# Seven products for two more pairs, and half of the layer norm on ScalarE: a fused FNet and GLU kernel on one core

## The chip, the core and the metric

The kernel runs on one core of one Trainium2 chip. Its engines work side by side, each through its own queue in order: TensorE (PE) multiplies, VectorE (DVE), ScalarE (ACT) and GpSimd (POOL) work on elements, SyncE (SP) and POOL issue DMAs, and 16 DMA engines carry those. The metric is the device time of one execution in microseconds (us); the time of a kernel is the median of its runs.

## The reference

All tensors are fp32.

```python
# S = 2048, D = 512, F = 1792
xn = layernorm(x)                                   # rows of 512, eps 1e-5, no weights
a, b = xn @ dft_hid_re.T, xn @ dft_hid_im.T
s = dft_seq_re @ a - dft_seq_im @ b
g = silu((sigmoid(xn @ w_gate) * (xn @ w_up)) @ w_down)
out = x + s * g
```

## The kernel before

All products are made of fp32 numbers split in two parts, hi and lo (`split`, L71 to L73: ACT copies the hi part, DVE subtracts it to get the lo part), and each product is three matmuls (`mm3`, L75): hi*hi, hi*lo, lo*hi. So an operand costs one ACT and one DVE instruction before PE can use it.

The work has three stages: the GLU with its gate (x by `w_gate` and `w_up`, then by `w_down`), the DFT along the sequence, and the DFT along the hidden dimension with the last product and sum. The change lies in the first.

The GLU works on the two halves h of the 2048 rows (1024 each) and on seven pairs g of F-columns (256 each). A **block** is one (h, g), in the order of `BLOCKS` (L27): after (0, 0), which is done while the first half is normalised, come (0,1), (0,2), (0,3), (0,4), (1,4) and so on. A block's product is done in Strassen's manner, as seven products in place of eight, and each of the seven is one **unit** of PE work: units 0 to 6 are block (0,1), 7 to 13 block (0,2), 14 to 20 block (0,3), 21 to 27 block (0,4), 28 to 34 block (1,4), the first one of the second half. A unit's 12 matmuls go to two banks of PSUM (ga and ua, or b and c), and after some units ACT copies the banks out (`snap`, `seed`) or DVE adds them (`plus`).

The product with `w_down` of a block's result (the **down product**) is done in pieces, each behind the main product of a unit of the next block. There are two ways. `Plain` (L314) has four pieces of 12 matmuls, and needs the weights and the four result tiles split. `Seven` (L388) has seven pieces of 6 matmuls, in Strassen's manner too, and needs four sums of results (`sums`), four differences of weights (`Down.diffs`), and seven results and two weight tiles split. The pieces of `Seven` lie in all seven units, from the second unit of the next block to the first of the one behind. Each piece ends in `gather` (L298): ACT copies its two banks into a page (L302), and POOL issues a DMA which adds the page to a tensor in DRAM (`g_part`, L304; the first one of each only writes, L307). Two of the seven go to `g_part` 0 one after the other, two to 2, two to 3. Pairs 1 and 2 of the first half are `Plain`, all others `Seven` (`SEVEN_FROM`, L987).

The layer norm of the second half's rows is made during the first blocks: `fetch` loads tiles 8 to 15 of 128 rows, two to a page; `norm_a` (L157) makes mean and variance on DVE (bn_stats, bn_aggr) and the scale on POOL; `norm_b` (L171) normalises the tile on DVE; `store_xn` (L197) stores it for the next stage, from POOL's queue. The GLU needs the second half turned, with rows along the free axis: `turned_half` (L175) stores mean and scale (`moments`) to DRAM from POOL's queue as single numbers (`store`, L183), loads them back spread over all partitions (`both`), and applies them to the turned x (`raw`, from `x_t`) on DVE in four steps of 128x1024 (`step`, L188).

What stands in the order: the program is written out unit by unit. `sooner(n, f)` puts f ahead of unit n, `after(n, f)` behind it; each unit's operands are loaded 5 units ahead and split 2 units ahead. Every engine then keeps that order. All tiles in SBUF are **pages** out of one pool of 54 slots of 4 KB per partition. Which slot a new page takes is fixed when the program is built; its first writer waits on the chip until the last reader of the page before it is done. For a page that was gathered, that reader is a DMA, and the wait ends when the DMA has landed.

Of the kernel before, what the change touches and what calls it, by code (L numbers as in the profile page):

```python
# [9 lines left out]
F32 = mybir.dt.float32  # L10
F32R = mybir.dt.float32r
AF = mybir.ActivationFunctionType
ALU = mybir.AluOpType
ADD, SUB = ALU.add, ALU.subtract

P = 128
S, D, F = 2048, 512, 1792
# [4 lines left out]
KH = NS // NH  # L22
NT = S // 512
SB = 512
EPS = 1e-5
# [1 line left out]
SCRATCH = 4096  # L27
BLOCKS = ((0, 1), (0, 2), (0, 3), (0, 4), (1, 4), (1, 5), (0, 5), (0, 6), (1, 6), (1, 0), (1, 1), (1, 2), (1, 3))
FIRST_TURNED = 1, 4
SEVEN_FROM = 3  # L30
SHARED = 4, 5, 6
SPLIT_AHEAD = 2
LOAD_AHEAD = 5
# [3 lines left out]
def fnet_glu_kernel(ctx: ExitStack, tc: tile.TileContext, x, x_t, c_re, c_im, w_h, w_gu, w_down, out):  # L37
    nc = tc.nc
    PSUM = bass.MemoryType.PSUM

    const = ctx.enter_context(tc.tile_pool(name="const", bufs=1))
# [5 lines left out]
    def page(shape, dtype=F32R):  # L47
        return pages.tile([P, *shape], dtype, name="page")

    def bank(tag):  # L50
        return banks.tile([P, 512], F32, name=tag, bufs=2 if tag == "pd" else 1)
# [5 lines left out]
    mhalf = const.tile([P, 1], F32, name="mhalf")  # L57
    nc.gpsimd.memset(mhalf, -0.5)
    warm = const.tile([P, 1], F32, name="warm")
    nc.scalar.activation(warm, mhalf, AF.Sigmoid)  # L60
    moments = const.tile([P, 2, KH], F32, name="moments")
    m_part = dram.tile([2, 2, SB], F32, name="m_part")
    xn_part = dram.tile([2, 2, 2, P, 4, D // 2], F32, name="xn_part")
    g_part = [dram.tile([P, 2, SB], F32, name=f"g_part{i}") for i in range(2 * NT)]
# [67 lines left out]
    def add(needs, run):  # L132
        units.append((needs, run))
# [4 lines left out]
    def after(n, f):  # L138
        extra.setdefault(n, []).append(f)

    def sooner(n, f):
        early.setdefault(n, []).append(f)


    xs = {}
# [7 lines left out]
            nc.sync.dma_start(xs[i + j], x[(i + j) * P : (i + j + 1) * P, :])  # L153

    st_of = {}

    def norm_a(i):  # L157
        st = stat.tile([P, 6], F32, name="st")
        mv = stat.tile([P, 2], F32, name="mv")
        rs = stat.tile([P, 2], F32, name="rs")  # L160
        nc.vector.bn_stats(st, xs[i])
        nc.vector.bn_aggr(mv, st)
        mean, scale = mv[:, 0:1], rs[:, 1:2]
        if i >= KH:
            mean, scale = (moments[:, m, i - KH : i - KH + 1] for m in range(2))
            nc.gpsimd.tensor_scalar(mean, mv[:, 0:1], 0.0, None, op0=ALU.add)
        nc.gpsimd.tensor_scalar(rs[:, 0:1], mv[:, 1:2], EPS, None, op0=ALU.add)
        nc.gpsimd.tensor_tensor(scale, rs[:, 0:1], mhalf, op=ALU.pow)
        st_of[i] = mean, scale

    def norm_b(i):  # L171
        mean, scale = st_of.pop(i)
        nc.vector.tensor_scalar(xs[i], xs[i], mean, scale, op0=ALU.subtract, op1=ALU.mult)

    def turned_half(n, b, at):  # L175

        both = Load(m_part[b].rearrange("m t -> (m t)").partition_broadcast(P).rearrange("p (m t) -> p m t", m=2), [2, SB])
        raw = [Load(x_t[(2 + b) * 2 + j], [2, SB]) for j in range(2)]

        def store():  # L180
            at = slice(b * SB // P, (b + 1) * SB // P)
            for m in range(2):
                nc.gpsimd.dma_start(m_part[b, m].rearrange("(o p) -> p o", p=P), moments[:, m, at])  # L183

        def step(j, m):
            v = xraw[1, j, b] = raw[j].load()
            by = both.load()[:, m, :].unsqueeze(1).to_broadcast([P, 2, SB])
            nc.vector.tensor_tensor(v, v, by, op=(SUB, ALU.mult)[m])  # L188

        after(n, store)  # L190
        sooner(at[0] - 2, both.load)
        for i in range(4):
            if i % 2 == 0:
                sooner(at[i] - 4, raw[i // 2].load)
            after(at[i], lambda i=i: step(*divmod(i, 2)))
# [118 lines left out]
    class Plain:  # L314


        items, at = range(4), (1, 3, 4, 6)
# [70 lines left out]
    class Seven:  # L388


        items, at = SEVEN, range(7)
# [52 lines left out]
    def block(h, w, made, before, job, late):  # L444

        s, ps = job.s, {}
        n = len(units)
        if not made:
            for i, v in zip((-3, 0, 1, 3), w["s"]):
                sooner(n + i, v.get)  # L450

        def snap(k):
            s[k] = page([2, SB], F32)
            for m, c in enumerate("gu"):
                nc.scalar.activation(s[k][:, m, :], ps[c + "a"], AF.Copy)

        def seed():

            for c in "gu":
                ps[c + "b"] = bank(c + "b")  # L460
                nc.scalar.activation(ps[c + "b"], ps[c + "a"], AF.Copy)

        def plus(k):
            for m, c in enumerate("gu"):
                nc.vector.tensor_add(s[k][:, m, :], s[k][:, m, :], ps[c + "c"])

        def gate(k, tag=None):
            if tag:
                s[k] = page([2, SB], F32)
            nc.scalar.activation(s[k][:, 0, :], ps["g" + tag] if tag else s[k][:, 0, :], AF.Sigmoid)  # L470

        def times(k, tag=None):
            nc.vector.tensor_mul(s[k][:, 0, :], s[k][:, 0, :], ps["u" + tag] if tag else s[k][:, 1, :])

        tail = {1: seed, 6: lambda: snap(2), 7: lambda: (snap(3), plus(3)), 3: lambda: plus(2)}
        CH = {1: "a", 5: "c", 2: "b", 6: "a", 7: "a", 4: "a", 3: "c"}

        def unit(k, d):
            first = k in (1, 5)
            for m, c in enumerate("gu"):  # L480
                tag = c + CH[k]
                if first:
                    ps[tag] = bank(tag)
                product(k, ps[tag], w, h, m, first)
            if k in tail:
                tail[k]()
            if d:
                d[0].run(d[1])
            if k in (2, 4):
                gate({2: 1, 4: 4}[k], CH[k])  # L490
            if k in (7, 3):
                gate({7: 3, 3: 2}[k])
            if k == 4:
                times(4, "a")

        for i, k in enumerate((1, 5, 2, 6, 7, 4, 3)):
            if i == 1:
                waiting.extend((before, d) for d in before.items)
            d = waiting.pop(0) if waiting and i in waiting[0][0].at else None
            add([xop[h, k], w[k]] + (d[0].needs(d[1]) if d else []), lambda k=k, d=d: unit(k, d))  # L500
        sooner(n + 3, lambda: times(1, "b"))
        sooner(n + 5, lambda: times(3))
        sooner(n + 7, lambda: times(2))
        job.spread(n, late)
        return job
# [470 lines left out]
    with tc.manual_schedule():  # L976
        job, begin = start(0, 0)
        for i in range(KH):
            after(i // 2, lambda i=i: store_xn(i))
        last = None  # L980
        for h, g in BLOCKS:
            made = g == last
            if not made:
                w, wd, last = w_operands(g), Down(g), g
            if (h, g) == FIRST_TURNED:
                turned_at = len(units)
            job = block(h, w, made, job, Seven(h, wd, made) if h or g >= SEVEN_FROM else Plain(h, g), g in SHARED)  # L987
        for i in range(0, KH, 2):
            a, b = ((2, 9), (4, 10), (7, 12), (8, 14))[i // 2]
            if i >= 4:  # L990
                sooner(a - 4, lambda i=i: fetch(KH + i))
            for j in (i, i + 1):
                after(a, lambda j=j: norm_a(KH + j))
                after(b, lambda j=j: norm_b(KH + j))
                after(b + 1, lambda j=j: store_xn(KH + j))
        n = turned_at
        turned_half(4, 0, (n - 18, n - 17, n - 14, n - 4))
        turned_half(8, 1, (n - 13, n - 12, n - 10, n - 3))
        for i, k in {-7: 1, -2: 2, 0: 3, 2: 4}.items():
            after(n + i, lambda k=k: x_sum(1, k))  # L1000
        for i, k in {-8: 1, -5: 5, -2: 2, 0: 6, 1: 7, 3: 4}.items():
            sooner(n + i, xop[1, k].get)
        sums_ahead(diffs, xn_blocks(0), s_part[0], (n + 15, n + 16, n + 17, n + 18), 3)
        sums_ahead(diffs, xn_blocks(1), s_part[1], (n + 28, n + 29, n + 30, n + 31), 3)
        sums_ahead(sums, c_blocks(0, 0), t_part[0], (n + 32, n + 33, n + 34, n + 35), 3)
        seq_units(job)
        hidden_units()
        begin()
        for n, (needs, run) in enumerate(units):
            now[0] = n  # L1010
            for f in early.get(n, []):
                f()
            for k in range(n, min(n + LOAD_AHEAD + 1, len(units))):
                for p in units[k][0]:
                    p.load()
            for k in range(n, min(n + SPLIT_AHEAD + 1, len(units))):
                for p in units[k][0]:
                    p.get()
            run()
            for f in extra.get(n, []):  # L1020
                f()
# [52 lines left out]
```

## Time and profile before

| | us |
|---|---|
| median of 3 runs | 813.05 (810.47 to 814.35) |
| profiled execution | 809.47 |
| its span, first to last instruction | 807.6 |
| PE busy | 801.0 (99%) |
| DVE busy | 639.7 (79%) |
| ACT busy | 496.9 (62%) |
| POOL busy | 150.8 (19%) |

The mean granted TensorE clock of the profiled execution is 0.999 of full speed. Busy time is the time in which an engine has an instruction under way; the share is of the span. A name such as page or g_part stands for all tiles of that name. The DMA share is the mean busy share of the 16 DMA engines, and it can pass 1, since an engine has several packets under way. The queue q0 holds what POOL issues, q1 what SP issues. "To landing" is the time from a DMA's issue to its last byte.

### The profile page before, as it was taken

Reading aid. Unit: us, or ns where it says so; the run is one execution under the profiler, and the core shown is the slowest. Engines: PE = TensorE matmul, PEld = TensorE weight load, DVE = VectorE, ACT = ScalarE, POOL = GpSimd, SP = SyncE. Lnnn points to the kernel's source line nnn. Section 1 sums busy time; section 2 is a strip of 40 time slices with the busy share of each in tenths; the row PEclk is TensorE's granted clock in tenths of the full one; section 3 lists DMA queues with packets and bytes.
Section 4 is the critical chain, followed back from the end, with each engine's and each line's share of the span. In section 5 each row is a group of like instructions: output and inputs, shape, how many; then the busy total and the mean of one; then the engine's idle time right before and its main releaser. Section 6 shows DMA issues by size and latency. Waiting matters only on the chain.

```text
span 807.6 us, 10288 instructions
## 1 busy us (share of the span) xinstructions
PE 801.0 (99%) x3630; PEld 665.3 (82%) x3630; DVE 639.7 (79%) x803; ACT 496.9 (62%) x761; POOL 150.8 (19%) x222
## 2 busy tenths in 40 slices
PE   9999999999999999999999999999999999999997
PEld 7988888888888888888888888888888888888886
DVE  6897879876776787787798796888888876986946
ACT  4674657777676678778877765445445545536360
POOL 3146321221222222131211100011101210001201
PEclk9999999999999999999999999999999999999999
DMA  8366994987899998989899988277929994799976
GB/s 278 140 225 110 219 263 72 182 159 156 240 253 226 290 295 236 236 199 175 236 294 311 282 294 293 98 284 286 329 85 324 350 389 141 244 337 386 314 254 104
DMA packets 55651, 193.62 MB, mean 240 GB/s; under 512 B 6320, under 2 KB 6576, under 8 KB 55600
## 3 DMA queue, kind: packets, MB, share of 16 engines
q0 software_dynamic: 24624, 85.48, 45.4%
q1 hardware_dynamic: 30896, 107.43, 37.7%
q8 instruction: 28, 0.46, 0.2%
q14 instruction: 23, 0.19, 0.1%
q10 hardware_dynamic: 80, 0.07, 0.0%
HBM read 110.62 MB, written 85.99 MB: 243 GB/s over the span
## 4 chain that ended last, share of the span: by engine, by line
PE 98%; DMA 1%; DVE 0%; ACT 0%; SPq 0%; issue 0%
PE pd L77 7%; PE pd L76 7%; PE pd L78 7%; PE ga L76 6%; PE ga L77 6%; PE ua L77 6%; PE ga L78 6%; PE ua L78 6%; PE ua L76 6%; PE gc L77 4%; PE uc L77 3%; PE gc L78 3%; PE uc L78 3%; PE gc L76 3%; PE uc L76 3%; PE ub L77 3%
## 5 line engine op out<-in xcount | busy, mean ns | idle before, releaser
L73 DVE TENSOR_TENSOR page<-page 128x1024 fp32r<-128x1024 f32 (+1 forms) x351 | 332.4, 976 | 110.3 <-ACT page L72 109.2
L72 ACT ACTIVATE page<-page 128x1024 fp32r<-128x1024 f32 (+1 forms) x351 | 284.2, 857 | 93.6 <-DVE page L124 74.2
L124 DVE TENSOR_TENSOR page<-page 128x1024 f32<-128x1024 f32 (+2 forms) x216 | 188.8, 893 | 0.9 <-DMA page<-in_w_gu_dram 0.3
L302 ACT ACTIVATE page<-pd 128x512 f32<-128x512 f32 x178 | 104.6, 598 | 67.5 <-PE pd L78 54.6
L304 POOL DMA_DIRECT2D g_part<-page x81 | 71.6, 949 | 282.5 <-ACT page L302 166.4
L76 PE MATMUL pd<-page 128*128 128x512 f32 x234 | 91.0, 389 | 0.0
L77 PE MATMUL pd<-page 128*128 128x512 f32 x234 | 91.0, 389 | 0.0
L78 PE MATMUL pd<-page 128*128 128x512 f32 x234 | 91.0, 389 | 0.0
L76 PE MATMUL ga<-page 128*128 128x512 f32 x200 | 78.2, 391 | 0.0
L77 PE MATMUL ga<-page 128*128 128x512 f32 x200 | 77.9, 389 | 0.0
L76 PE MATMUL ua<-page 128*128 128x512 f32 x200 | 77.8, 389 | 0.0
L77 PE MATMUL ua<-page 128*128 128x512 f32 x200 | 77.8, 389 | 0.0
L78 PE MATMUL ga<-page 128*128 128x512 f32 x200 | 77.8, 389 | 0.0
L78 PE MATMUL ua<-page 128*128 128x512 f32 x200 | 77.8, 389 | 0.0
L76 PEld LDWEIGHTS pd<-page 128*128 128x128 f32 x234 | 43.9, 188 | 9.2
L78 PEld LDWEIGHTS pd<-page 128*128 128x128 f32 x234 | 43.9, 188 | 9.1
L77 PEld LDWEIGHTS pd<-page 128*128 128x128 f32 x234 | 43.9, 188 | 9.1
L77 PE MATMUL gc<-page 128*128 128x512 f32 x124 | 48.3, 390 | 0.0
L76 PE MATMUL gc<-page 128*128 128x512 f32 x124 | 48.2, 389 | 0.0
L78 PE MATMUL gc<-page 128*128 128x512 f32 x124 | 48.2, 389 | 0.0
L76 PE MATMUL uc<-page 128*128 128x512 f32 x124 | 48.2, 389 | 0.0
L78 PE MATMUL uc<-page 128*128 128x512 f32 x124 | 48.2, 389 | 0.0
(133 smaller groups left out, 1302.3 us busy)
## 6 DMA issues: line engine op xcount, KB each, us to landing
g_part<-page POOLq DMA_DIRECT2D x89, 512.0 KB, 8.3
page<-f_part SPq DMA_DIRECT2D x36, 512.0 KB, 6.1
page<-in_c_re_dram SPq DMA_DIRECT2D x34, 512.0 KB, 6.2
page<-in_c_im_dram SPq DMA_DIRECT2D x33, 512.0 KB, 7.0
f_part<-page POOLq DMA_DIRECT2D x28, 512.0 KB, 6.9
page<-in_w_gu_dram SPq DMA_DIRECT2D x22, 512.0 KB, 7.0
page<-xn_part SPq DMA_DIRECT2D x14, 512.0 KB, 5.6
page<-in_w_down_dram SPq DMA_DIRECT2D x11, 512.0 KB, 7.9
```

The costliest lines, as they stand in the source:

```text
L72: nc.scalar.activation(hi, src, AF.Copy)
L73: nc.vector.tensor_tensor(lo, src, hi.bitcast(F32), op=SUB)
L76: nc.tensor.matmul(ps, ws[0], ms[0], start=first, stop=False, skip_group_check=go_on)
L77: nc.tensor.matmul(ps, ws[0], ms[1], start=False, stop=False, skip_group_check=go_on)
L78: nc.tensor.matmul(ps, ws[1], ms[0], start=False, stop=last, skip_group_check=go_on)
L124: (engine or nc.vector).tensor_tensor(dst, a, b, op=op)
L302: nc.scalar.activation(pg[:, o, :], po, AF.Copy, scale=float(sign))
L304: nc.gpsimd.dma_start(g_part[i], pg, accum_op=ADD)
```

## The change

Pairs 1 and 2 of the first half become `Seven` too (`SEVENS`). The statistics of tiles 8 to 15 are made by ACT in two passes with a running sum, each 128x512 and written to a page that nobody reads: the sum (from which POOL makes mean and minus mean), then the sum of the squared differences (from which POOL makes scale and minus mean times scale). The tiles are normalised by ACT with scale and bias. The passes come a unit or two sooner than the statistics did, normalising and storing come later (tiles 8 and 9 after unit 11, not 9; 10 and 11 after 14, not 10; 12 and 13 after 28, not 12; 14 and 15 after 30, not 14), and the steps of `turned_half` move: units 10, 11, 12, 13 in place of 10, 11, 14, 24, and 15, 17, 22, 24 in place of 15, 16, 18, 25. Lines behind L27 stand up to 18 lines lower in the changed file: L302 and L304 become L319 and L321.

```diff
-SEVEN_FROM = 3
+SEVENS = 1, 2, 3, 4, 5, 6
...
-    moments = const.tile([P, 2, KH], F32, name="moments")
+    moments = const.tile([P, 6, KH], F32, name="moments")
...
+    unused = Value([], lambda: page([D], F32))
...
         mean, scale = mv[:, 0:1], rs[:, 1:2]
-        if i >= KH:
-            mean, scale = (moments[:, m, i - KH : i - KH + 1] for m in range(2))
-            nc.gpsimd.tensor_scalar(mean, mv[:, 0:1], 0.0, None, op0=ALU.add)
         nc.gpsimd.tensor_scalar(rs[:, 0:1], mv[:, 1:2], EPS, None, op0=ALU.add)
         nc.gpsimd.tensor_tensor(scale, rs[:, 0:1], mhalf, op=ALU.pow)
         st_of[i] = mean, scale
+
+    def second_stats(i, m):
+
+        def at(k):
+            return moments[:, k, i - KH : i - KH + 1]
+
+        if m == 0:
+            nc.scalar.activation(unused.get(), xs[i], AF.Identity, accum_out=at(2))
+            nc.gpsimd.tensor_scalar(at(0), at(2), 1.0 / D, None, op0=ALU.mult)
+            nc.gpsimd.tensor_scalar(at(3), at(2), -1.0 / D, None, op0=ALU.mult)
+        else:
+            nc.scalar.activation(unused.get(), xs[i], AF.Square, bias=at(3), accum_out=at(4))
+            nc.gpsimd.tensor_scalar(at(4), at(4), 1.0 / D, EPS, op0=ALU.mult, op1=ALU.add)
+            nc.gpsimd.tensor_tensor(at(1), at(4), mhalf, op=ALU.pow)
+            nc.gpsimd.tensor_tensor(at(5), at(3), at(1), op=ALU.mult)
+
+    def second_norm(i):
+        scale, bias = (moments[:, m, i - KH : i - KH + 1] for m in (1, 5))
+        nc.scalar.activation(xs[i], xs[i], AF.Identity, scale=scale, bias=bias)
...
-            job = block(h, w, made, job, Seven(h, wd, made) if h or g >= SEVEN_FROM else Plain(h, g), g in SHARED)
+            job = block(h, w, made, job, Seven(h, wd, made) if h or g in SEVENS else Plain(h, g), g in SHARED)
         for i in range(0, KH, 2):
-            a, b = ((2, 9), (4, 10), (7, 12), (8, 14))[i // 2]
+            a, b = ((1, 11), (3, 14), (5, 28), (7, 30))[i // 2]
             if i >= 4:
                 sooner(a - 4, lambda i=i: fetch(KH + i))
             for j in (i, i + 1):
-                after(a, lambda j=j: norm_a(KH + j))
-                after(b, lambda j=j: norm_b(KH + j))
+                after(a, lambda j=j: second_stats(KH + j, 0))
+                after(a + 1, lambda j=j: second_stats(KH + j, 1))
+                after(b, lambda j=j: second_norm(KH + j))
                 after(b + 1, lambda j=j: store_xn(KH + j))
         n = turned_at
-        turned_half(4, 0, (n - 18, n - 17, n - 14, n - 4))
-        turned_half(8, 1, (n - 13, n - 12, n - 10, n - 3))
+        turned_half(4, 0, (n - 18, n - 17, n - 16, n - 15))
+        turned_half(8, 1, (n - 13, n - 11, n - 6, n - 4))
```

## The prediction

> **What bounds the kernel now.** I read the page's first lines, then the chain that ended last, then the waits of PE's weight loads and of ACT, and last the windows of the GLU's first blocks.
>
> ```profile
> span 807.6 us, 10288 instructions
> PE 801.0 (99%) x3630; PEld 665.3 (82%) x3630; DVE 639.7 (79%) x803; ACT 496.9 (62%) x761; POOL 150.8 (19%) x222
> ...
> PE 98%; DMA 1%; DVE 0%; ACT 0%; SPq 0%; issue 0%
> ```
>
> PE is busy for 801.0 of 807.6 us and carries 98% of the chain. The waits say the same: those of PE's weight loads in the GLU are few and small (here us, times, longest).
>
> ```profile
> PEld ga L76 <- ACT page L455: 1.1, 3, 0.5
> PEld gc L77 <- DVE page L73: 0.4, 1, 0.4
> ```
>
> So a change moves the time in two ways only: by the number of matmuls, or by making an operand late. An engine with time to spare, as DVE and ACT have over the span, earns nothing when it is relieved. Whether an operand comes late is read block by block. The windows are blocks (0,1), (0,2), (0,3) and (0,4) of the kernel before, then a short stretch in which one gather runs.
>
> ```profile
> core 0: us, PE busy (x) PEld busy (x) DVE busy (x) ACT busy (x) POOL busy (x), PEclk, DMA share, GB/s
> 35.48:65.30 29.82, 29.81 (x133) 24.35 (x132) 26.26 (x39) 19.93 (x33) 12.59 (x23) 1.00 0.46 159
> 65.30:95.20 29.90, 29.90 (x133) 24.76 (x132) 22.15 (x39) 17.16 (x30) 14.20 (x22) 1.00 0.92 155
> 95.20:125.10 29.90, 29.90 (x133) 24.77 (x132) 24.39 (x37) 18.31 (x31) 6.50 (x8) 1.00 0.90 250
> 125.10:153.40 28.30, 28.30 (x126) 23.44 (x125) 24.75 (x38) 21.94 (x38) 5.15 (x6) 1.00 0.67 105
> 128.00:132.00 4.00, 4.00 (x20) 3.30 (x19) 4.00 (x7) 1.56 (x4) 0.00 (x0) 1.00 0.84 131
> ```
>
> In each block PE has no gap. DVE has 3.5 to 7.8 us to spare, ACT 6 to 13. The DMA engines have the least in blocks (0,2) and (0,3): a share of 0.92 and 0.90.
>
> **Matmuls: -2.72 us.** A Plain down product has four pieces of 12 matmuls, a Seven seven of 6: 48 against 42, for two pairs 12 fewer. Twelve matmuls in a row, by the starts of the first and of the one behind the last:
>
> ```profile
> 54.86 0.39 PE L76 MATMUL pd<-page 128*128 128x512 f32 x1
> ...
> 57.58 0.39 PE L76 MATMUL ga<-page 128*128 128x512 f32 x1
> ...
> 65.74 0.39 PE L76 MATMUL ga<-page 128*128 128x512 f32 x1
> ```
>
> That is 2.72 us, 0.227 each. All of it is on the path, since PE is dense. The same pitch gives the deadlines of the changed kernel: unit 7 starts at 65.74 as before, has no piece and takes 2.72; each later unit, with a piece of 6, takes 18 matmuls, 4.08 us. So unit 8 starts at 68.46, unit 9 at 72.54, unit 12 at 84.78, unit 14 at 92.94, and the piece of unit 14 at 95.66.
>
> **DVE: nothing.** It loses statistics and normalising, and gains sums and differences for two pairs.
>
> ```profile
> L161 DVE BATCH_NORM_STATS2 st<-page 128x6 f32<-128x512 f32 x16 | 10.9, 680 | 2.1 <-DMA page<-in_x_dram 2.0
> L162 DVE BATCH_NORM_AGGREGATE mv<-st 128x2 f32<-128x6 f32 x16 | 2.9, 182 | 0.8
> L173 DVE TENSOR_SCALAR page<-page,moments 128x512 f32<-128x512 f32 x8 | 4.0, 544 | 0.0
> L73 DVE TENSOR_TENSOR page<-page 128x1024 fp32r<-128x1024 f32 x190 | 227.6, 1221 | 88.9 <-ACT page L72 88.2 <-DMA g_part<-page 0.4
> L124 DVE TENSOR_TENSOR page<-page 128x512 f32<-128x512 f32 x84 | 55.9, 686 | 0.6 <-DMA page<-in_w_gu_dram 0.3
> ```
>
> Eight tiles of the second half give back 8 x (0.680 + 0.182 + 0.544) = 11.2 us. A Seven pair adds, beside the splits, four sums (0.686 each) and its weight differences; the kernel before has that load in block (0,4), after pair 3 went over to Seven, and DVE there is at 24.75 of 28.30. I estimate 24 to 26 us of work in each block. PE hides that; no cost.
>
> **ACT: tight, no cost in the sum.** It gains the statistics, the normalising, more copies of PSUM and more splits.
>
> ```profile
> L302 ACT ACTIVATE page<-pd 128x512 f32<-128x512 f32 x178 | 104.6, 598 | 67.5 <-PE pd L78 54.6 <-issue 4.3 <-DMA g_part<-page 3.1
> L72 ACT ACTIVATE page<-page 128x512 fp32r<-128x512 f32 x161 | 95.7, 626 | 25.9 <-DVE page L124 18.3 <-DVE page L473 6.1 <-DVE page L548 1.5
> L72 ACT ACTIVATE page<-page 128x1024 fp32r<-128x1024 f32 x190 | 192.0, 1053 | 67.8 <-DVE page L124 55.9 <-issue 5.0 <-DVE page L247 2.3
> L168 POOL TENSOR_TENSOR moments<-rs,mhalf 128x1 f32<-128x1 f32 x8 | 5.2, 646 | 0.7
> ```
>
> A pass of 128x512 with a running sum is not in this trace. The nearest rows are plain ACT instructions of that shape, 0.598 and 0.626; the pass writes as much and adds up besides, and all passes write one page, each behind the other. From above I bound it by the row of twice the size, 1.053, and take 0.70, near the rows of the same shape. Below 0.598 it will not go, since the elements are as many. Block (0,1) gets 12 passes, 8.4 us, and one split of weight differences, 1.05: 19.93 + 9.45 = 29.4 of its 29.8 us. Block (0,2): 17.16 + 4 passes 2.8 + 2 normalised tiles 1.3 + 4 copies 2.4 + 3 splits of results 1.9 + 1.05 = 26.6 in 27.2 us (the 29.90 less 2.72). Block (0,3): 18.31 + 2 x 0.63 + 6 x 0.6 + 3 x 0.63 = 25.1 in 28.6. It fits everywhere, with 0.4 us to spare at the worst place; the 16 short POOL instructions added, of 0.646 each, 10.3 us in all, fit into POOL's free time.
>
> **DMA: the term that decides.** A Seven pair gathers seven times in place of four.
>
> ```profile
> q1 hardware_dynamic: 30896, 107.43, 37.7%
> ```
>
> The stretch 128 to 132 prices one adding gather at 4.00 x 0.84 = 3.36 us of all 16 engines. Block (0,2) gets three more and loses two stores of normalised tiles (an estimate of 0.74 each: by this row of the page, 37.7% of 807.6 us for 107.43 MB, 256 KB take that): 0.92 x 29.90 = 27.5, plus 10.1, minus 1.5, makes 36 us of DMA work in 27.2 us. Block (0,3): 26.9 + 10.1 - 1.5 = 35.5 in 28.6. So some 16 us of transfers don't fit where they are issued, and landings move back. Block (0,4), at 0.67, can take up much of it. What this costs depends on who waits for a landing.
>
> ```profile
> L304 POOL DMA_DIRECT2D g_part<-page x2: 913/924/935, 83.2 to 88.7; - x2
> ...
> DMA to landing us min/median/max: 14.6/14.6/14.6
> L304 POOL DMA_DIRECT2D g_part<-page x7: 843/859/1529, 269.1 to 293.1; - x7
> ...
> DMA to landing us min/median/max: 5.5/10.2/14.7
> L304 POOL DMA_DIRECT2D g_part<-page x3: 852/864/907, 113.2 to 126.7; - x3
> ...
> DMA to landing us min/median/max: 5.2/5.4/5.9
> L183 POOL DMA_DIRECT2D m_part<-moments x4: 764/804/863, 62.3 to 80.4; - x4
> ...
> DMA to landing us min/median/max: 12.7/12.8/12.9
> 85.00:90.00 5.00, 5.00 (x24) 4.14 (x23) 5.00 (x9) 2.82 (x5) 1.92 (x3) 1.00 0.94 70
> ```
>
> The first pair of rows is the gathers issued at 83 to 89 us: 14.6 us to landing, with the engines at 0.94 for only 70 GB/s from 85 to 90. Those are the stores of the moments, single numbers of four bytes, the last issued at 80.4. The second pair of rows is seven gathers of a later Seven block, the third the quickest ones.
>
> In the changed kernel, as its instructions are built, three waits follow from this. The page into which ACT copies a PSUM bank in unit 11 was gathered by unit 8. Unit 9's gather adds to the same `g_part` as unit 8's and must wait for that landing, with POOL's whole queue behind it (stores of moments, units 10 and 11's gathers). ACT's copy for unit 13's gather goes into the page that unit 10's gather read, and PE's piece in unit 14 needs that copy's PSUM bank free. On ACT, all splits queue behind such a copy.
>
> Unit 8's piece ends at 72.54; two copies of 0.598 put its gather at 73.7. Among the moments, the second pair of which is issued at about 77, I give it the 14.6 us seen: it lands at 88.3. Unit 12's operands, due at 84.78, are then about 3.5 us late, since ACT stood at the copy in unit 11. Then POOL issues units 9 and 10's gathers, 0.92 us for the first, and both run beside loads:
>
> ```profile
> q0 software_dynamic: 89, 0.31, 59.1%
> q1 hardware_dynamic: 95, 0.35, 44.6%
> ```
>
> From 100 to 102 us, with work on both queues, POOL's queue had 59.1% of the engines' time: 2 x 3.36 / 0.591 = 11.4 us. They land at 100.6, ACT's copy ends at 101.2, and PE's piece due at 95.66 is 5.56 us late, the 3.5 included. [...]
>
> Ends of this term: with 10.2 us for unit 8's gather and 2 x 5.4 (the quickest rows) for the others, it lands 95.3 and nothing is lost; with 14.6, and 15.6 for two in flight (14.7 and one issue), it is 103.9, plus 0.6, 8.8 us late.
>
> **The sum.** -2.72 + 5.56 = +2.84. The profiled execution took 809.47, 3.6 below the median of the runs, 813.05, and below the lowest of them; against its own time the changed kernel comes to 812.3, against the median to 815.9. I forecast 815.9, with 811.5 to 819.2 as this case's own range (a stall of 1.2 to 8.8). What a measurement can tell from no change is about 0.5%, 4.07 us: 809.0 to 817.1.
>
> **Rivals.** First, the cover holds: the gathers land within 13.6 us of their issue, or the 54 pages give ACT room, and PE loses only matmuls: 813.05 - 2.72 = 810.3, a little less if the 0.4 us wait for DVE goes too. For it: from 266 to 295 us a Seven pair runs with landings of up to 14.7 and PE waits for none of them. Against: there no moments are stored, and no normalised tiles. It decides if unit 8's gather lands by about 83. Chance 0.30.
>
> Second, ACT becomes the bound of block (0,1): if a pass takes 1.053 in place of 0.70, the block needs 19.93 + 1.05 + 12 x 1.053 = 33.6 us in 29.8, and PE ends 3.8 late: 814.1 without a late gather. It decides from 0.73 us a pass on. For it: 0.4 us of room. Against: the rows of the shape are near 0.6. [...] Chance 0.14.
>
> Third, the 16 us of DMA work run on: block (0,4)'s loads come late as well, and only one unit's lead, 4.1 us, is taken off: 813.05 - 2.72 + 11.7 = 822.0. Against: loads go five units ahead. Chance 0.08.
>
> **How the numbers follow.** The forecast has 0.48. Under 809.0 ends only a part of the first rival, 0.06. Over 817.1 ends about a third of the forecast's range, 0.17, a little of the second rival, 0.02, and the third, 0.08: 0.27. The rest, 0.67, is within 0.5%. The range goes from the first rival's 810.3 less the small waits of a microsecond, 809.3, to 821.0, short of the third.
>
> **What would show it.** PE's busy time 2.7 us lower, or I counted wrong. Right: waits of PE or its loads for ACT's copies or splits between 84 and 104 us, of ACT for DMA g_part, 5 to 6 us together, and gathers of units 8 to 10 that take over 13 us to land. Wrong: PE without a gap from 65 to 125 us (first rival); passes of over 0.73 us and waits for ACT before 72 us (second); waits for loads of weights behind 125 us (third). A wait elsewhere, by DVE above all, would be one that I have not seen.

## The result and the profile after

The changed kernel takes 820.16 us (818.87 to 821.74, six runs), the kernel before in the same comparison 811.76 (809.53 to 814.35): a ratio of 1.0115, 95% interval 1.0095 to 1.0136. A second comparison gave 819.57 against 810.89, 1.0103 (1.0070 to 1.0135). So the change costs 8 to 9 us where 2.84 were forecast (from 813.05 to 815.9), and it lies above the 0.5% that the forecast set for "no change".

The first lines of the profile after, and of its chain that ended last:

```profile
span 819.8 us, 10350 instructions
PE 801.4 (98%) x3618; PEld 661.6 (81%) x3618; DVE 644.5 (79%) x803; ACT 520.4 (63%) x821; POOL 164.8 (20%) x244
...
PE 74%; DMA 17%; ACT 3%; DVE 3%; issue 2%; POOL 1%; SPq 0%; POOLq 0%; DVEq 0%; ACTq 0%
```

DVE's and ACT's shares of the span have hardly moved, which says nothing; the chain does: 17% of it now runs through DMAs, where 1% did. PE has 12 instructions fewer, and it waits. Its waits, one by one, from the timeline of PE after (start, duration, and in brackets the idle time and what ended it; only rows with a wait are copied, and around the first long one the row before it and the one behind it):

```profile
52.55 0.50 PE L76 MATMUL ga<-page 128*128 128x512 f32 x1 [0.48 <-ACT page L472]
85.10 0.39 PE L78 MATMUL pd<-page 128*128 128x512 f32 x1
88.03 0.50 PE L76 MATMUL ga<-page 128*128 128x512 f32 x1 [2.54 <-ACT page L472]
88.37 0.40 PE L77 MATMUL ga<-page 128*128 128x512 f32 x1
...
94.88 0.50 PE L76 MATMUL gc<-page 128*128 128x512 f32 x1 [2.43 <-DVE page L482]
98.48 0.50 PE L76 MATMUL pd<-page 128*128 128x512 f32 x1 [0.58 <-ACT page L319]
104.59 0.50 PE L76 MATMUL gc<-page 128*128 128x512 f32 x1 [0.38 <-DVE page L482]
118.26 0.50 PE L76 MATMUL ga<-page 128*128 128x512 f32 x1 [0.47 <-ACT page L472]
177.20 0.50 PE L76 MATMUL ga<-page 128*128 128x512 f32 x1 [1.22 <-ACT page L472]
```

Three more follow later: 0.78 at 325 us, 1.74 and 0.76 at 449 and 450 us. A wait costs more than its bracket. Without one, the matmul at 88.03 would have begun at 85.10 + 0.23 = 85.33, and the next at 85.56; that one began at 88.37, 2.81 late, where the bracket says 2.54. So this restart adds 0.27, and I take the same for the others. The ten waits are 11.4 us, the restarts 2.7, the matmuls saved 2.7: 11.4 against a span that is 12.2 longer; 0.8 is not accounted for. The four waits from 85 to 105 us are 5.9 us and 1.1 for restarts, the largest part.

What releases PE in both long cases goes back to the landing of a DMA. From the timelines of ACT, POOL and DVE:

```profile
87.38 0.60 ACT L472 ACTIVATE page<-ga 128x512 f32<-128x512 f32 x1 [3.35 <-DMA g_part<-page]
87.86 2.73 POOL L321 DMA_DIRECT2D g_part<-page  x3 [6.79 <-DMA g_part<-page]
92.33 0.69 DVE L124 TENSOR_TENSOR page<-page 128x512 f32<-128x512 f32 x1 [6.95 <-DMA page<-in_w_gu_dram]
```

How long these transfers took, first the gathers by the time of their issue (unit 8's, then those of units 9, 10 and 11), then the gate weights, with the us to landing:

```profile
L321 POOL DMA_DIRECT2D g_part<-page x1: 967/967/967, 74.9 to 74.9; - x1
...
DMA to landing us min/median/max: 12.4/12.4/12.4
L321 POOL DMA_DIRECT2D g_part<-page x3: 852/914/1221, 87.9 to 89.7; - x3
...
DMA to landing us min/median/max: 9.9/11.5/13.2
L87 SPq DMA_DIRECT2D page<-in_w_gu_dram x2: 371/377/383, 75.0 to 75.5; - x2
...
DMA to landing us min/median/max: 8.8/12.8/16.8
```

Unit 8's gather was issued at 74.9; its landing let ACT copy at 87.4 and POOL issue the next gathers at 87.9. The second load of gate weights landed at 92.3, and DVE stood at the difference that reads it.

**The same kernel a second time:**

> The changed kernel as it is, for a second profile. If the 3.3 us lost at 449 us in its first profile belong to the change, they are there again; if they are what single runs of any of these kernels lose at the start of the next stage, they differ, and the stalls at 52, 88, 95, 118 and 177 us stay. Time 820, as before.

Nothing is lost at 449 us in this profile (817.44 us), and the short waits at 53 (0.48) and 177 us (1.23) are there again; the one at 118 us is not. The large loss has another form. The gather landed 15.4 us after issue, and PE waited once, and long (timeline of PE):

```profile
91.28 0.80 PE L76 MATMUL ga<-page 128*128 128x512 f32 x1 [5.56 <-ACT page L472]
91.87 0.63 PE L77 MATMUL ga<-page 128*128 128x512 f32 x1
...
97.30 0.39 PE L78 MATMUL pd<-page 128*128 128x512 f32 x1
```

The windows of the same stretch, with the granted clock in the column PEclk:

```profile
core 0: us, PE busy (x) PEld busy (x) DVE busy (x) ACT busy (x) POOL busy (x), PEclk, DMA share, GB/s
91.00:93.00 2.00, 1.72 (x4) 1.44 (x5) 1.83 (x4) 1.69 (x4) 1.82 (x3) 0.50 0.74 168
95.00:97.00 2.00, 2.00 (x7) 1.52 (x6) 1.70 (x4) 1.78 (x4) 0.00 (x0) 0.50 1.06 258
97.00:105.00 8.00, 8.00 (x36) 6.64 (x35) 5.80 (x8) 5.13 (x9) 2.44 (x4) 0.99 1.04 216
```

After 5.56 us of standing still the granted clock is 0.50 until about 97 us: 13 matmuls start 0.43 apart in place of 0.227, 13 x 0.20 = 2.6 us more, in which PE is "busy" and nothing waits.

### The profile page after: what moved, and what is told of

It reads as the page before. It is cut to its first block, busy times and chain, and to the rows that moved or that the text cites. A ratio compares the mean times of both kernels' runs of the same rounds, so it can differ in the third digit from the quotient of the medians.

```text
span 819.8 us, 10350 instructions
## 1 busy us (share of the span) xinstructions
PE 801.4 (98%) x3618; PEld 661.6 (81%) x3618; DVE 644.5 (79%) x803; ACT 520.4 (63%) x821; POOL 164.8 (20%) x244
## 4 chain that ended last, share of the span: by engine, by line
PE 74%; DMA 17%; ACT 3%; DVE 3%; issue 2%; POOL 1%; SPq 0%; POOLq 0%; DVEq 0%; ACTq 0%
DMA g_part<-page 9%; DMA page<-in_w_gu_dram 4%; PE ga L76 4%; PE ga L77 4%; PE ga L78 4%; PE ua L76 4%; PE ua L78 4%; PE ua L77 4%; PE pd L77 4%; PE pd L76 4%; PE pd L78 4%; PE ub L78 3%; PE ub L76 3%; PE ub L77 3%; PE gb L78 3%; PE gb L76 3%
## 5 line engine op out<-in xcount | busy, mean ns | idle before, releaser
L73 DVE TENSOR_TENSOR page<-page 128x1024 fp32r<-128x1024 f32 (+1 forms) x359 | 338.2, 972 | 113.5 <-ACT page L72 110.4
L72 ACT ACTIVATE page<-page 128x1024 fp32r<-128x1024 f32 (+1 forms) x359 | 290.6, 855 | 99.5 <-DVE page L124 71.9
L124 DVE TENSOR_TENSOR page<-page 128x1024 f32<-128x1024 f32 (+2 forms) x232 | 196.6, 869 | 11.2 <-DMA page<-in_w_gu_dram 10.4
L319 ACT ACTIVATE page<-pd 128x512 f32<-128x512 f32 x190 | 108.8, 598 | 42.6 <-PE pd L78 29.9
L321 POOL DMA_DIRECT2D g_part<-page x87 | 77.5, 999 | 289.5 <-ACT page L319 169.9
L76 PE MATMUL pd<-page 128*128 128x512 f32 x230 | 89.8, 390 | 0.7 <-ACT page L319 0.6
L77 PE MATMUL pd<-page 128*128 128x512 f32 x230 | 89.5, 389 | 0.0
L78 PE MATMUL pd<-page 128*128 128x512 f32 x230 | 89.5, 389 | 0.0
L76 PEld LDWEIGHTS ga<-page 128*128 128x128 f32 x200 | 37.5, 188 | 18.4 <-ACT page L472 8.8
L76 PEld LDWEIGHTS pd<-page 128*128 128x128 f32 x230 | 43.2, 188 | 10.8 <-ACT page L319 1.9
L78 PEld LDWEIGHTS pd<-page 128*128 128x128 f32 x230 | 43.2, 188 | 9.0
L77 PEld LDWEIGHTS pd<-page 128*128 128x128 f32 x230 | 43.2, 188 | 8.9
L76 PE MATMUL uc<-page 128*128 128x512 f32 x124 | 48.3, 389 | 0.0
```

Of the source, the lines that this page charges most:

```text
L72: nc.scalar.activation(hi, src, AF.Copy)
L73: nc.vector.tensor_tensor(lo, src, hi.bitcast(F32), op=SUB)
L76: nc.tensor.matmul(ps, ws[0], ms[0], start=first, stop=False, skip_group_check=go_on)
L77: nc.tensor.matmul(ps, ws[0], ms[1], start=False, stop=False, skip_group_check=go_on)
L78: nc.tensor.matmul(ps, ws[1], ms[0], start=False, stop=last, skip_group_check=go_on)
L124: (engine or nc.vector).tensor_tensor(dst, a, b, op=op)
```

## The experiments

Each time is the median of its runs; the ratio is against the kernel before in the same comparison (810.1 to 810.9), with its 95% interval.

### One half of the change at a time

```diff
-SEVEN_FROM = 3
+SEVEN_FROM = 1
```

> Edit: the kernel before with pairs 1 and 2 of the first half as Seven; statistics, normalising, stores and the order of the turned half as before. Theory A (the forecast's: the earlier Seven pairs put gathers onto DMA engines that the stores of the moments hold; landings come late): most of the loss between 84 and 105 us stays, though the changed kernel's loss at 52 us (0.5 us) goes; 816 to 820 us. Theory B (ACT's statistics cause it): no stall, only 12 matmuls fewer, 2.7 us faster than before. Theory C (neither alone; the moved loads of the turned half make it): a part, 810 to 815.

819.59 us, ratio 1.0102 (1.0077 to 1.0126). The Seven pairs alone cost as much as the whole change; PE waited 1.56 us at 82.5 and 5.59 at 92.5, again with a clock of 0.50 behind it, and 1.58 at 122. Theory A's number, though the waits at 82 and 122 us are of another kind: they come again below where the collision is gone.

```diff
-SEVENS = 1, 2, 3, 4, 5, 6
+SEVENS = 3, 4, 5, 6
```

> Edit: the changed kernel with pairs 1 and 2 of the first half left Plain; everything on ScalarE and every moved step as in the change. Theory A: within 0.2% of the kernel before, at most 0.8 us slower by the short stall at 52 us. Theory B: it carries the loss, 818 to 823 us. Theory C: some of the loss, 2 to 5 us, from a load of gate weights that lands late behind an x_t load moved ahead of it.

814.77 us, 1.0043 (1.0029 to 1.0058). That is none of A's 0.8 us: theory C's range. So the statistics on ScalarE, with the steps that moved along, cost some 4 us by themselves, and the halves don't add up: 9.2 and 4.4 alone, 8 to 9 together. PE's longest wait in this run, beside 0.47 at 53 and 1.21 at 174 us (timeline of PE):

```profile
93.21 0.50 PE L76 MATMUL gc<-page 128*128 128x512 f32 x1 [2.16 <-DVE page L482]
```

### The stores of the moments

```diff
-nc.gpsimd.dma_start(m_part[b, m].rearrange("(o p) -> p o", p=P), moments[:, m, at])
+nc.gpsimd.dma_start(m_part[b, m].rearrange("(p o) -> p o", p=P), moments[:, m, at])
```

> Edit: the changed kernel, but the stores of the moments write four numbers of a partition side by side, 128 pieces of 16 bytes in place of 512 of 4 (mean and scale then stand at other rows: the output differs; the work is the same). Theory A: stores land in about 3 to 6 us in place of 12 to 13, unit 8's gather lands before 83 us, the stalls at 88 and 95 us are gone or under 1 us: 6 us or more faster than the changed kernel. Theory B: no difference. Theory C: the stall at 88 goes, the one at 95 stays (2.4 us).

811.46 us, 1.0013 (0.9997 to 1.0028): 8.7 us under the changed kernel, by the shape of four stores of 2 KB. Between 60 and 120 us PE waited 0.19 and 0.47 us. Landings in this run, of the moments (the two loads of them included) and of unit 8's gather:

```profile
L200 POOL DMA_DIRECT2D m_part<-moments x4: 540/596/642, 63.2 to 80.2; - x4
L87 SPq DMA_DIRECT2D page<-m_part x2: 327/327/327, 66.8 to 84.3; - x2
DMA to landing us min/median/max: 1.8/4.2/7.0
...
L321 POOL DMA_DIRECT2D g_part<-page x1: 961/961/961, 75.1 to 75.1; - x1
DMA to landing us min/median/max: 7.4/7.4/7.4
```

The gather takes 7.4 us in place of 12.4 to 15.4, and the stores and loads of the moments 1.8 to 7.0, where in the changed kernel the second two stores alone took 12.2 and 12.7. So the form of these stores is the cause of the larger part, shown by changing it alone. No row here counts the pieces: 512 and 128 are the program's, and the profile after lists 64 packets under 512 bytes from 62 to 74 us, where two of the 512-piece stores lie.

The form of the stores can act in two ways, and this run takes both away. Their pieces are in flight beside the gather. And SP's queue stands still: its load of `m_part` waits until the first moments have landed (73.95 in the changed kernel, 10.1 us behind an issue that took from 63.01 to 63.85), and every load behind it in the queue waits too (timeline of SP, changed kernel):

```profile
74.08 0.33 SPq L87 DMA_DIRECT2D page<-m_part  x1
```

With 16-byte pieces this load is issued at 66.8 (the row above). In the changed kernel six loads of 512 KB go out from 74.1 to 77.4, around unit 8's gather at 74.9; with 16-byte pieces five of the six were out by 68.6. How much of the gather's delay each of the two ways makes is not shown. The kernel before has the same hold (74.0).

```diff
 def gather(...):
     (ACT copies as before)
+    (return here for the first piece of pair 1: unit 8's DMA is not issued)
```

> Edit: the changed kernel without one DMA, the gather of the first of the seven pieces of pair 1 (its two ACT copies stay; the product is missing from the sum). Theory A: unit 9's gather does not wait and ACT's copy in unit 11 does not either, so the stall of 2.5 us at 88 us is gone; the one at 95 us shrinks by the 3.4 us of DMA work that is gone or stays. In all 3 to 6 us faster than the changed kernel. Theory B: no difference. Theory C: 2.5 us faster, the stall at 95 us stays.

812.61 us, 1.0024 (1.0009 to 1.0039), 7.5 us under the changed kernel. The waits at 88 and 95 us are both gone, and the gate weights landed in 7.2 us at most, with the x_t load still ahead of them. A wait of 0.87 is left at 99 us, in unit 15, where the changed kernel has 0.38 at 104.59. So both long waits hang on one gather among the stores of the moments. That is more than A's 3 to 6, which counted neither restarts nor, as in the second profile, the time at half clock.

### Does Seven pay once the stores are out of the way?

```diff
 (Seven alone, 16-byte stores, and so that all values stay at their rows:)
-by = both.load()[:, m, :].unsqueeze(1).to_broadcast([P, 2, SB])
-nc.vector.tensor_tensor(v, v, by, op=(SUB, ALU.mult)[m])
+by = both.load()[:, m, :].rearrange("p (q o) -> p o q", o=SB // P)
+for k in range(2):
+    vk = v[:, k, :].rearrange("p (o q) -> p o q", o=SB // P)
+    nc.vector.tensor_tensor(vk, vk, by, op=(SUB, ALU.mult)[m])
```

> Edit: the kernel before with pairs 1 and 2 as Seven, and the stores of the moments as 16-byte pieces with the rows kept right (the steps of the turned half read the loaded numbers through a view that puts them in order, each step as two instructions of 128x512). Theory A (four-byte stores and the earlier gathers collide, the rest of a Seven pair fits): the 9 us that Seven alone lost come back and the 12 matmuls show, 2 to 3 us faster than the kernel before, about 807.5. Theory D (Seven's own gathers and loads are too much for the DMA engines there, whatever the stores): still 2 us or more slower than before.

817.77 us, 1.0071 (1.0047 to 1.0094). A's 807.5 failed, but D isn't shown by it, since the edit brought a cost of its own: read through that view, a step of 128x512 took 1.078 us on DVE, two of them 2.16, where one of 128x1024 takes 1.22. Eight steps are 7.5 us more for DVE, and DVE was busy without a gap from 115.5 to 118.8 us, while PE waited 3.01.

```diff
 (Seven alone and 16-byte stores at other rows, without the view)
```

> Edit: pairs 1 and 2 as Seven with the statistics on VectorE, and the moments stored as 16-byte pieces at other rows (the output differs), without the view that made the steps of the turned half slow on VectorE. Theory A (only the collision of the four-byte stores costs): 2 to 3 us faster than before, about 808. Theory G (the collision is gone, but without the change's other half VectorE is the bound there: it has the statistics, the normalising and a Seven pair's sums in the same 40 us): 812 to 816, with PE waiting for VectorE or for ACT behind it between 90 and 125 us.

813.12 us, 1.0022 (1.0005 to 1.0039): theory G. Unit 8's gather landed in 8.5 us and 12 matmuls are saved, and yet the kernel is slower than before. A window of this run (columns as in the windows above):

```profile
85.00:105.00 20.00, 19.73 (x86) 15.69 (x85) 19.82 (x31) 12.95 (x25) 9.60 (x12) 1.00 0.94 235
```

PE waited 1.49 us at 82, 1.01 at 108 and 1.60 at 115, each time for ACT. DVE is busy 19.82 of the 20.00 us in the window, and ACT's splits at 77.6 and 81.2 had waited for DVE. In the run with 16-byte stores and the whole change the same stretch had 18.70. So the two halves of the change belong together: without ScalarE's statistics, DVE is the bound here once two more pairs are Seven.

```diff
 (the kernel before with the 16-byte stores and the view, pairs 1 and 2 Plain)
```

> Edit: the kernel before with nothing but the 16-byte stores of the moments and the view that reads them. All theories that need the earlier Seven pairs for the loss: no difference from the kernel before (within 0.1%), since PE there waits for nothing. If the four-byte stores cost the kernel before something by themselves: faster by 1 us or more.

811.26 us, 1.0004 (0.9982 to 1.0025): no difference. The four-byte stores are in the kernel before at the same time, 79.5 us, and cost it nothing there; they cost where a Seven pair's gathers wait among them. Its profiled run (816.4 us) lost several us from 435 to 447, with waits like those at 449 above (1.75 and 0.76): the profiles of several of these kernels have that, the second one of the change has not.

### A form of the stores with all values in place

```diff
+nc.vector.transpose(turned_moments[:, b, :], moments[:, b, :])   # 128x32
+for k in range(4):
+    to = m_part[b].rearrange("m (o k i) -> k (m o) i", k=4, i=32)[k]
+    nc.gpsimd.dma_start(to, turned_moments[32 * k : 32 * k + 8, b, :])
```

> Edit: the whole change, with the moments of a half turned on VectorE (one 32x32-block transpose of 128x32, two units behind the old place) and stored as rows of 128 bytes from 32 partitions, four DMAs a half; all values stand where they belong. Theory A: as the 16-byte form did in the change, 811 to 812, no stall over 0.6 us between 80 and 110 us. If it was the count of DMAs on POOL's queue, not their small pieces: no better than the change, 820.

813.92 us, 1.0047 (1.0025 to 1.0069): 6 us of the loss come back, not 8.7, and no wait from 80 to 110 us is over 0.51 us. The transpose took 0.20 us. What the other 2.5 us are isn't settled: there are eight DMAs in place of four, two units later, and SP's queue stood until 75.9 us. Unit 8's gather, issued at 75.8, landed in 9.9 us where the 16-byte form had 7.4. No store of moments was in flight beside it, but SP's loads were; so the loads can account for some of the 12.4 to 15.4, and the pieces of the stores for the rest. That is argued from these rows, not shown by a run that changes one alone.

```diff
 (on top of that)
-a, b = ((1, 11), (3, 14), (5, 28), (7, 30))[i // 2]
+a, b = ((1, 11), (3, 14), (5, 18), (7, 21))[i // 2]
-after(a, ... second_stats(KH + j, 0)); after(a + 1, ... second_stats(KH + j, 1))
+after(j + 1, ... second_stats(KH + j, 0)); after(j + 2, ... second_stats(KH + j, 1))
```

> Edit: as the run with turned moments, but each tile's two passes lie one tile a unit (first pass of tile 8 in unit 1, second in unit 2, tile 9 one unit on, and so on), and tiles 12 to 15 are normalised in units 18 and 21 in place of 28 and 30. Theory E (what is left are two short stalls of ACT's order, 0.5 us at 53 us where a second pass waits for POOL, and 1.2 us at 172 us where normalising in unit 30 stands ahead of splits): both go, 809 to 810, a little faster than before. Otherwise they come back in other units: 811 or more.

814.50 us, 1.0044 (1.0022 to 1.0066). The waits at 53 (0.20 left of 0.48) and 172 us went as theory E had it, but one of 0.76 came at 83, one of 0.21 in unit 13 grew to 0.58, and 0.45 at 114 stayed. Nothing was gained.

### The steps that moved along

```diff
-turned_half(4, 0, (n - 18, n - 17, n - 16, n - 15))
-turned_half(8, 1, (n - 13, n - 11, n - 6, n - 4))
+turned_half(4, 0, (n - 18, n - 17, n - 14, n - 4))
+turned_half(8, 1, (n - 13, n - 12, n - 10, n - 3))
```

> Edit: pairs 1 and 2 Plain, statistics and normalising on ScalarE as in the change, but the steps of the turned half (and with them their loads) at the units of the kernel before. Theory E (the x_t load moved ahead of the gate weights makes these land late): the stall of 2.2 us at 93 us goes, the short ones at 53 and 174 us stay: 812 to 813. Theory F (it is ScalarE's order that stalls PE there): the stall stays, 814 to 815.

811.76 us (pairs 1 and 2 Plain), 1.0020 (0.9996 to 1.0043): theory E, a little under its 812 to 813. The wait of 2.16 us at 93 us is gone, those at 53 and 171 us stay. Gate weights to landing, with the change's steps (statistics alone):

```profile
DMA to landing us min/median/max: 7.7/11.7/15.6
```

and with the old ones:

```profile
DMA to landing us min/median/max: 6.2/6.9/7.6
```

The x_t load ahead of them in SP's queue was the difference, in a queue that in both runs stands until about 74 us for the moments.

> Edit: the whole change, four-byte stores and all, but the steps of the turned half with their loads at the units of the kernel before. Theory E (the x_t load moved ahead of the gate weights makes them land at 92 us): the stall of 2.4 us at 95 us goes, that of 2.5 us at 88 us stays: 816 to 818. If the collision alone decides: no difference from the change, 820.

820.10 us, 1.0123 (1.0086 to 1.0161): in the whole change the same edit brings nothing. The gate weights landed in 8.4 us at most and the wait at 95 us went, but PE's other waits grew (timeline of PE):

```profile
88.93 0.50 PE L76 MATMUL ga<-page 128*128 128x512 f32 x1 [3.26 <-ACT page L472]
102.26 0.50 PE L76 MATMUL pd<-page 128*128 128x512 f32 x1 [2.14 <-ACT page L319]
```

The first is unit 12, behind unit 8's gather. The second is the piece of unit 14, for an ACT copy that waited 1.79 us for the landing of a later gather. At 117.55 PE waited 1.26 more, of the kind that pair 2 alone shows below. So the two waits that go back to unit 8's gather are 5.4 us without any late gate weights.

```diff
-nc.scalar.activation(xs[i], xs[i], AF.Identity, scale=scale, bias=bias)
+nc.vector.tensor_scalar(xs[i], xs[i], mean, scale, op0=ALU.subtract, op1=ALU.mult)
```

> Edit: pairs 1 and 2 Plain, statistics on ScalarE as in the change, tiles 8 to 15 normalised on VectorE instead of ScalarE, at the change's units. Theory E (ScalarE's normalising in unit 30 stands ahead of splits that PE needs): the stall of 1.2 us at 174 us goes, the rest stays: 813 to 814. Other theory (the DMA or the splits themselves are late there): no difference, 814.8.

815.27 us, 1.0059 (1.0034 to 1.0085). Theory E failed: the wait at 172 us stayed, 1.50 us. It is not ScalarE that makes it but the place. In unit 30 DVE normalised instead, 1.00 us, ahead of the difference at 168.81 (1.22 us), and ACT's next split began at 170.12, when that was done. Moved out of units 28 and 30, as in the run with the passes spread, the normalising costs no wait there.

### Which pair

```diff
 (first run: the kernel before; second and third run: the change)
-SEVEN_FROM = 3
+SEVEN_FROM = 2
-SEVENS = 1, 2, 3, 4, 5, 6
+SEVENS = 2, 3, 4, 5, 6
```

> Edit: the kernel before with pair 2 alone as Seven too (pair 1 stays Plain), statistics on VectorE, four-byte stores. Theory A: pair 2's gathers are issued from 95 us on, behind the last moments (landed at 92 us), so they meet nothing: 6 matmuls less, 1.4 us, 809 to 810, or level with before if VectorE is late once. If it is the DMA load of any earlier Seven pair: 813 or more, with stalls from 95 to 125 us.

810.50 us, 1.0001 (0.9982 to 1.0020). Between 85 and 110 us PE waits for nothing: the collision needs pair 1. One wait is left, and a step on DVE stands ahead of it (timelines of PE and DVE):

```profile
112.43 0.50 PE L76 MATMUL ga<-page 128*128 128x512 f32 x1 [1.49 <-ACT page L455]
...
109.41 1.22 DVE L188 TENSOR_TENSOR page<-page 128x1024 f32<-128x1024 f32 x1
```

> Edit: the whole change, with pair 1 left Plain. Theory A: the stall at 88 us goes; that at 93 us (late gate weights, 2.2 us in the run of the statistics alone) and the short ones at 53 and 172 us stay, and 1.4 us of matmuls go: 813 to 814. Otherwise stalls over 1 us between 95 and 125 us: 816 or more.

814.90 us, 1.0066 (1.0046 to 1.0087): the wait at 88 us is gone, 1.62 us at 93, 0.48 at 53, 0.52 at 114 and 1.21 at 173 stay. The matmuls that pair 2 saves as Seven didn't pay for them.

> Edit: as the run before it (pair 1 Plain, the rest of the change), with the steps of the turned half at the units of the kernel before, each tile's two passes one tile a unit, tiles 12 to 15 normalised in units 18 and 21, and the moments of both halves stored one unit later. Theory A and E together: no stall over 0.5 us between 50 and 180 us, 809 to 810, a little under before. If ScalarE's load stalls PE wherever it lies: 811 to 813.

810.10 us, 1.0006 (0.9988 to 1.0024): level with before, and not without stalls as forecast. For the waits at 53 and 173 us, which are gone, it was the place and not the load. 1.49 us at 92 and 1.40 at 114 are left. At 92 DVE again waited for gate weights, though the x_t load was back at its old place: with the stores one unit later SP's queue stood until 75.8 us, and the second load, issued at 76.7, landed 13.2 us later. The one at 114 is where the step in unit 18 stood in the run with pair 2 alone.

```diff
 (pair 2 alone as Seven, statistics on VectorE)
-turned_half(8, 1, (n - 13, n - 12, n - 10, n - 3))
+turned_half(8, 1, (n - 13, n - 11, n - 6, n - 4))
```

> Edit: pair 2 alone as Seven, statistics on VectorE, and from the change only the places of the turned half's second steps (units 15, 17, 22 and 24 in place of 15, 16, 18 and 25). If the stall of 1.5 us at 112 us is VectorE's step in unit 18, which stands ahead of differences that ScalarE and then PE wait for, it goes and the 6 matmuls show: 1.4 us under the kernel before, 808.7 to 809.3. If VectorE's load stalls PE there wherever the step lies: level with before, 810.5.

809.47 us against 810.89, ratio 0.9985 (0.9971 to 1.0000). The wait at 112 us is down from 1.49 to 0.31. This is the one version under the kernel before, by 1.4 us, the price of the six matmuls, at the edge of what can be measured.

## Why the prediction was right and wrong

Two terms of the sum failed: the DMA term was too small, and ACT, put at nothing, cost 2.2 us.

**Matmuls** (-2.72): as counted. PE has 12 instructions fewer, and the version that lost nearly nothing elsewhere gained 1.4 us from six. The sign set for it, PE's busy time 2.7 us lower, did not come: 801.4 against 801.0, since ten restarts of 0.27, 2.7 us, count as busy.

**DMA, the mechanism**: right, and nearly to the place. Unit 8's gather was put at 73.7 and its landing at 88.3; it was issued at 74.9 and let ACT and POOL go on at 87.4 to 87.9 (at 90.6 in the second profile). ACT's copy in unit 11, POOL's queue and PE at unit 12 waited as listed. Giving the stores larger pieces, or leaving out that one gather, brought 8.7 and 7.5 us back. The prediction did not have SP's queue, which the same stores hold.

**DMA, the size**: 5.56 us were forecast; 7.0 and 8.4 came. From 85 to 105 us it was 5.9 of waits and 1.1 of restarts in the first profile; in the second 5.56 of one wait, 0.3 for its restart and 2.6 at half clock, 8.4. That this one wait has the forecast's figure is luck: the forecast had 3.5 of it at unit 12 and 2.0 at the piece of unit 14. The working moved all later work by the wait alone, without restarts or a lower clock. And it named one late landing where there were two: it did not follow the loads of the steps that the change moves. An x_t load now stands ahead of the gate weights, which landed 16.8 us after issue. With Plain pairs that costs 3 us by itself (814.77 against 811.76). Where the steps stay at their old units, the change's waits are nearly those of the forecast: 3.26 at unit 12 and 2.14 at the piece of unit 14.

**Units 9 and 10's gathers**: right as far as ACT. Forecast to land at 100.6 after 11.4 us, they and unit 11's took 9.9 to 13.2 from 87.9 to 89.7 on, and ACT's copy waited for a landing until 101.7. But PE's piece in unit 14, at 102.7, waited for nothing: PE had by then been held up twice, the second time by the gate weights. The 0.58 at 98 us is the piece of unit 13.

**ACT, no cost**: wrong, but not by the price of a pass, taken at 0.70 us. The groups of the profile after:

```profile
L186 ACT ACTIVATE page<-page,moments 128x512 f32<-128x512 f32 x8 | 6.1, 812 | 0.0
L179 ACT ACTIVATE page<-page,moments 128x512 f32<-128x512 f32 x8 | 5.8, 722 | 1.3 <-POOL moments L177 1.0
L175 ACT ACTIVATE page<-page 128x512 f32<-128x512 f32 x8 | 5.0, 630 | 0.1
```

L175 takes no operand from a column, L179 one (the bias), L186 two (scale and bias); their means are 630, 722 and 812 ns, 92 and 90 apart. That the columns make the difference is read from these rows, not shown by a run that changes them alone. The running sum needs one more instruction of 0.19 us to read it out, so the durations of a pass add up to 0.82 or 0.91. But neighbouring instructions overlap by about 0.1 (timeline of ACT; the window of block (0,1) below it, columns as above):

```profile
48.82 0.73 ACT L179 ACTIVATE page<-page,moments 128x512 f32<-128x512 f32 x1 [0.96 <-POOL moments L177]
...
60.23 0.72 ACT L179 ACTIVATE page<-page,moments 128x512 f32<-128x512 f32 x1
60.86 0.19 ACT L179 ACTIVATION_READ_ACCUMULATOR page<-page,moments 128x1 f32 x1
60.96 0.61 ACT L72 ACTIVATE page<-page 128x512 fp32r<-128x512 f32 x1
...
35.48:65.30 29.82, 29.34 (x128) 23.63 (x127) 23.40 (x32) 25.77 (x52) 17.52 (x34) 1.00 0.42 155
```

A pass with its read-out holds ACT for 0.73 us, from 60.23 to 60.96, and ACT is busy for 25.77 of 29.82 us where 29.4 were forecast. ACT had time to spare in the block; two places broke even so. At 53 us PE waited 0.48, because a second pass had stood 0.96 for the mean that POOL makes, ahead of copies that PE needed. At 177 us it waited 1.22, by the normalising in unit 30, outside the three blocks that were added up at all. That is 1.7 us, 2.2 with restarts. The sum over a block hid them.

**DVE, nothing**: nearly right for the whole change, and only for it. Seven without the statistics on ScalarE fills DVE. The 0.47 at 118 us in the first profile is not ACT's term: with both pairs Plain and the statistics on ScalarE there is no such wait, and with pair 2 as Seven and the statistics on VectorE there are 1.49, behind a step on DVE; 0.31 is left when the step moves.

**The sum**, with what the runs showed: -2.7, +7.0 from 85 to 105 us, +2.2 for ACT, +0.7 at 118 us, 7.3 us in the first profile; -2.7, +8.4, +2.2, 8.0 in the second. The medians differ by 8.4 and 8.7. What was lost at 325 and 449 us in the first profile is not in it: the second has neither.

**Rivals**: the cover that holds failed; where the prediction took it from, 266 to 295 us, no moments are stored, as was said against it. The backlog into later blocks wasn't seen. The second rival, ACT as the bound of block (0,1), did not come true; what ACT cost was a matter of order and belonged in the sum. Two smaller workings are off, with nothing in the sum resting on them: the best case of the DMA term leaves out the 0.92 us of an issue and would end 0.6 us late, not in time; and block (0,2) gets two more gathers of pair 1, not three, since the seventh piece lies in unit 14.

## What to carry to other kernels

Add up an engine's load between two neighbouring deadlines, not over a block: a spare microsecond in the mean does not help the one place where a new instruction stands ahead of a split. When a transfer is moved or added, look for small-piece transfers in flight beside it, and for queues that wait for them, and change their shape first; here four stores of 2 KB in 4-byte pieces cost 8.7 us. And price a stall with what follows it: the restart, here 0.27 us, and the time at a lower clock, here 2.6 us more at 0.50.

## What the runs showed of the hardware that was not expected

- A stall of 5.56 us was followed by 5.7 us at a granted clock of 0.50, 2.6 us more; stalls of 2.54 and 3.26 us by none, at 1.00. The length alone does not decide: behind 3.01 us in the run of Seven with the view the clock was 0.98 from 118 to 120 us and 0.50 from 120 to 122; behind 1.10 and 0.76 us with one matmul between them, in the run without unit 8's gather, the matmul at 442.91 us took 0.63, as those at 0.50 did. What else decides is not shown.
- A store of 512 four-byte pieces took 12.2 to 12.7 us to land in the changed kernel (the second two); with 128 pieces of 16 bytes the stores and loads of the moments took 1.8 to 7.0, and the gather of 512 KB beside it 7.4 in place of 12.4 to 15.4. While the first stores were in flight SP's queue issued nothing until 74.1 us; with 16-byte pieces it went on at 66.8.
- An operand that DVE reads at a step of 16 bytes made a 128x512 subtraction or product take 1.078 us; a 128x1024 one read in order takes 1.22.
